# First weights transformed by kind, the gate's transfer issued behind the first fold, and four sums ahead of two folds

## The chip, the cores and the metric

The kernel runs on one core of a Trainium2 chip. The metric is the device time of one execution in microseconds (us); smaller is better. The core has five engines that run in parallel, each with its own instruction queue worked through in order: TensorE (PE, matrix products into the PSUM memory), VectorE (DVE), ScalarE (ACT), GpSimd (POOL) and SyncE (SP, which here only issues transfers). DMA transfers are issued by SP, ACT or POOL and are carried out by 16 DMA engines that all issuers share.

## The reference

```python
def _attn_ref(x):                     # x: (8, 3008, 256) f32
    X = np.fft.fft(x, axis=1)
    X = np.fft.fft(X, axis=2)
    return X.real.astype(np.float32)

def _moe_ref(x, w_gate, w_val, w_out):  # (24064, 256), two (256, 1536), (1536, 256)
    g = x @ w_gate
    silu = g * (1.0 / (1.0 + np.exp(-g)))
    val = x @ w_val
    return (silu * val @ w_out).astype(np.float32)
```

The real part of a two-dimensional Fourier transform of each of 8 sequences is flattened to 24,064 rows and goes through a gated feed-forward block (SwiGLU) with inner width 1536.

## The kernel before, in words

The transform along the 256 columns is moved into the weights: the gate and value weights are multiplied once by a cosine table (`CD`) and a sine table (`SDt`). This gives `Wp` (cosine kind) and `Wq` (sine kind), and `Wm`, which is `Wq` scaled by `m2` for the mirrored rows. The transform along the 3008 rows is done on PE with tables `Tab`, after the rows have been "folded": rows and columns that share a cosine or sine are added or subtracted first. Its results are the tiles `Pt` and `Qt`. Then the long steady loop takes `Pt` and `Qt` through `Wp`, `Wq` and `Wm` (line 1337 on PE), SiLU and products on ACT, DVE and POOL, and the output weights (line 1599 on PE). The order of that loop is fixed by a planner when the kernel is built; it is the same whatever happens before it. The change lies in the code ahead of the loop, which is written out by hand in the order of the queues; it prepares the first sequence and the first 512 of the 1536 columns of the gate and value weights.

The first sequence is loaded in two chunks: a long one (`XA`, 128 row groups) and a short one (`XC0`, 60 row groups twice). SP and ACT issue the loads of x; POOL issues the weights, which are cast to bf16 on the way.

- `load_w` (lines 394 and 396): four transfers issued by POOL. `load_w(1, (0,))` is the first 512 columns of the gate into `W0[0]`, `load_w(1, (1,))` those of val into `W0[1]`, and `load_w(0)` the other 1024 columns of both into the space of `XA`.
- `place` (line 444): PE brings rows into order; `sums` (line 453): DVE adds or subtracts these and the rows that fall, into `SA` (long chunk) and `SC` (short chunk).
- `fold_d` (lines 511, 512): POOL folds `SA` over the columns, one quarter of it a call, and ACT casts the result to `EOb`. `fold_c` (line 507): DVE folds `SC` into `EB` (named `EOf` in the profile).
- `half_folded` (line 497) and `folded_c` (line 503): PE accumulates the first transform out of the long and the short chunk into four accumulators: `eo` 0 gives `Pt`, 1 gives `Qt`, each with one in a `v` and one in a `g` slot of PSUM. `row0` (line 611) adds single rows to those of `Qt`.
- `transform` (lines 642, 647): ACT copies one accumulator, and DVE adds and subtracts it from the other into `Pt` or `Qt`.
- `half_w` (lines 473, 475, 477): the first 512 weight columns in two halves of 256. A call makes one kind (cosine or sine) for gate and val together: four products into one PSUM tile of the `o` slots, and one copy, on ACT or (second half, cosine kind) on DVE. `double` (line 481): ACT makes `Wm` of one half.
- `weight_op` (lines 1805, 1808, 1811, 1814): the first operations of the loop that need the other 1024 columns.
- `opposite` (line 383), `weigh_ce` (line 386): ACT finishes tables. `turns` (line 363, POOL) and `angles` (line 367, DVE) start the tables for a later part. At line 669 ACT clears a small tile that SP then writes into the empty rows of `XC` (line 671).

PSUM has 8 slots: three named `g`, three `v`, two `o`; each kind is handed out in turn ahead of the loop, and by the planner inside it.

Of the kernel before, what the change touches and what calls it, by code (L numbers as in the profile page):

```python
# [12 lines left out]
F32 = mybir.dt.float32  # L13
I32 = mybir.dt.int32
BF16 = mybir.dt.bfloat16
AF = mybir.ActivationFunctionType
# [15 lines left out]
def kernel(  # L32
# [8 lines left out]
    nc = tc.nc  # L41
    B, M, D = x.shape
    Dff = moe_w_gate.shape[1]
    P = 128
# [5 lines left out]
    T = 512  # L50
# [42 lines left out]
    psG = Slots("psG", 3, space=bass.MemoryType.PSUM)  # L93
    psV = Slots("psV", 3, space=bass.MemoryType.PSUM)
    psO = Slots("psO", 2, space=bass.MemoryType.PSUM)
    ctx.enter_context(tc.manual_schedule())

    Wp = const.tile([P, 2, Dff], BF16, name="Wp")
    Wq = const.tile([P, 2, Dff], BF16, name="Wq")
    Wm = const.tile([P, 2, Dff], BF16, name="Wm")  # L100
# [6 lines left out]
    CD = const.tile([P, 2, P], BF16, name="CD")  # L107
    SDt = const.tile([P, 2, P], BF16, name="SDt")
    m2 = const.tile([P, 1], F32, name="m2")
# [135 lines left out]
    SC = tq.tile([P, 2, 2, 2, D], F32, name="SC")  # L245
    SA = tp.tile([P, 2, 4, 2, D], F32, name="SA")
    EOb = tp.tile([P, 2, 4, 2, P], BF16, name="EOb")
    XC0 = tp.tile([P, 4, 2, D], F32, name="XC0")
    W0 = [tp.tile([P, 2, T], BF16, name=f"W0{i}") for i in range(2)]
# [8 lines left out]
    q = nc.sync  # L258
# [48 lines left out]
    for i in range(4):  # L307
        ps = psO.tile([P, T], F32, name="o")
# [46 lines left out]
    def row_signs():  # L355
        pts(sgo, pc, scalar1=float(NCR), scalar2=-2.0, op0=Alu.is_equal, op1=Alu.mult)
        pts(sgo, sgo, scalar1=1.0, scalar2=sgn, op0=Alu.add, op1=Alu.mult)
# [18 lines left out]
    def cosine(ch, lo, hi, ra):  # L376
        nc.scalar.activation(Tab[:, ch, :, 0, lo:hi], ra, AF.Sin, scale=-sc, bias=halfpi)
# [4 lines left out]
    def opposite(ch):  # L382
        nc.scalar.activation(Tab[:, ch, :, :, NCE:NOO - 1], Tab[:, ch, :, :, GH + 1:NCE], AF.Copy, scale=-1.0)
# [4 lines left out]
    def load_w(first, only=(0, 1)):  # L388
        for i, src in ((0, moe_w_gate), (1, moe_w_val)):
            if i not in only:  # L390
                continue
            w_ = src.rearrange("(no p) f -> p no f", p=P)
            if first:
                nc.gpsimd.dma_start(out=W0[i], in_=w_[:, :, 0:T])
            else:
                nc.gpsimd.dma_start(out=Wraw[i][:, :, 0:Dff - T], in_=w_[:, :, T:Dff])
# [13 lines left out]
    nc.gpsimd.memset(EOf[:, 1, :, P:P + 1], 0.0)  # L410
    nc.gpsimd.memset(sel[0:1, :], 1.0)
    row_signs()
    load_w(1, (0,))


    ce_angle = [[tp.tile([P, 2, NCE], F32, name=f"{nm}{ch}") for nm in ("rr", "ra")] for ch in range(2)]
# [32 lines left out]
    def sums(S, k, X, pss, only=None):  # L449
        n = len(pss)  # L450
        for a in only or range(n):
            down = X[:, 7 - a] if n == 4 else X[:, 2 + a]
            vtt(S[:, k, a], pss[a], down[:, ::-1, :], op=(Alu.add, Alu.subtract)[k])
# [10 lines left out]
        for i in range(n):  # L464
            nc.tensor.matmul(ps[:, 0:P], sel, sel, start=True, stop=True)

    def half_w(h, k, pool, nm):
        ps = pool.tile([P, 2, T // 2], F32, name=nm)
        dst, tab = ((Wp, CD), (Wq, SDt))[k]
        fs = slice(h * T // 2, (h + 1) * T // 2)  # L470
        for gv in range(2):
            for no in range(2):
                nc.tensor.matmul(ps[:, gv, :], tab[:, no, :], W0[gv][:, no, fs], start=(no == 0), stop=(no == 1))
        if k or not h:
            nc.scalar.copy(dst[:, :, fs], ps)
        else:
            nc.vector.tensor_copy(dst[:, :, fs], ps)

    def double(h):
        fs = slice(h * T // 2, (h + 1) * T // 2)  # L480
        nc.scalar.activation(Wm[:, :, fs], Wq[:, :, fs], AF.Copy, scale=m2)

    def start_acc(eo):
        for q, (pool, nm) in enumerate(((psV, "v"), (psG, "g"))):
            acc[eo][q] = pool.tile([P, T], F32, name=nm)

    def set_cols(ps, tab, a):
        if a % 2:
            return (ps[:, 0:2 * GH + 2].rearrange("p (t n) -> p t n", t=2),
                    tab[:, 0:2 * NCE].rearrange("p (t n) -> p t n", t=2)[:, :, 0:GH + 1])  # L490
        return ps[:, 0:NCE], tab[:, 0:NCE]

    def half_folded(eo, a0):
        for q in range(2):
            for a in range(a0, a0 + 2):
                dst, rhs = set_cols(acc[eo][q], Tab[:, 0, q, eo], a)
                nc.tensor.matmul(dst, EOb[:, eo, a, q, :], rhs, start=(a == 0), stop=False, skip_group_check=True)

    def folded_c(eo):
        for a in range(2):  # L500
            for q in range(2):
                dst, rhs = set_cols(acc[eo][q], Tab[:, 1, q, eo], a)
                nc.tensor.matmul(dst, EB[:, eo, a, q, :], rhs, start=False, stop=a == 1, skip_group_check=True)

# [4 lines left out]
    def fold_d(eo, a0):  # L509
        s_ = SA[:, eo, a0:a0 + 2]  # L510
        ptt(EOA[:, eo, a0:a0 + 2, :, 0:P], s_[:, :, :, P:0:-1], s_[:, :, :, P:D], op=(Alu.add, Alu.subtract)[eo])
        nc.scalar.copy(EOb[:, eo, a0:a0 + 2], EOA[:, eo, a0:a0 + 2, :, 0:P])
# [34 lines left out]
    start_acc(1)  # L547
    start_acc(0)
    fold_d(0, 0)
    cosine(1, 0, NCE, ce_angle[1][1])  # L550
    half_folded(0, 0)
    psC = place(XC0, putC, 2, ((psO, "o"),))
# [6 lines left out]
    load_w(0)  # L559
    opposite(1)  # L560
    half_folded(0, 2)
    half_folded(1, 2)
    for k, a in ((0, 0), (1, 0), (0, 1)):
        sums(SC, k, XC0, psC, (a,))
    fold_c(0)
    sums(SC, 1, XC0, psC, (1,))
    fold_c(1)
    X3c = XC.rearrange("p a q d -> p (a q d)")
    hd = tp.tile([P, 2, 2, 1], F32, name="hd")
# [31 lines left out]
    def row0(b, q, ps):  # L601
        CE = coef_a(b)[0]
        if b:
            for k, (c, e) in enumerate(((0, E0), (0, E1), (1, slice(0, NCE)))):
                nc.tensor.matmul(ps[:, e], Z0[:, q, k, :], Tab[:, c, q, 0, e], start=False, stop=True,  # L605
                                 skip_group_check=True)
            return
        todo = [(CE[:, q, 0, k, P:P + 1], Tab[:, 0, q, 0, e], e) for k, e in ((0, E0), (1, E1))]
        todo += [(CEc[:, q, 0, k, 0:1], Tab[:, 1, q, 0, e], e) for k, e in ((0, E0), (1, E1))]
        for l, r_, cols in todo:  # L610
            nc.tensor.matmul(ps[0:1, cols], l, r_, start=False, stop=True, skip_group_check=True)
# [11 lines left out]
    def transform(b, part, eos, given=None):  # L623
        n = NCE if part == 0 else G
        ev, ods = {}, {}
        for q, pool, nm in ((0, psO, "o"), (1, psG, "g")):
            if given:
                ps = {eo: given[eo][q] for eo in eos}
            else:
                ps = {eo: pool.tile([P, T], F32, name=nm) for eo in eos}  # L630
                for eo in eos:
                    mms = products(b, part, q, eo)
                    for i, (l, r_, cols) in enumerate(mms):
                        nc.tensor.matmul(ps[eo][:, cols], l, r_, start=(i == 0), stop=(i == len(mms) - 1),
                                         skip_group_check=True)
            if part == 0 and 1 in eos and not given:

                row0(b, q, ps[1])
            for eo in eos:
                if q == 0:  # L640
                    ods[eo] = odp.tile([P, NCE], F32, name="od")
                    nc.scalar.copy(ods[eo][:, 0:n], ps[eo][:, 0:n])
                else:
                    ev[eo] = ps[eo]

        def put(eo, dst, s0, w, minus):
            nc.vector.tensor_tensor(dst, ev[eo][:, s0:s0 + w], ods[eo][:, s0:s0 + w],
                                    op=Alu.subtract if minus else Alu.add)

        if part == 0:  # L650
            runs = [(0, GH, 1, 0), (GH, GH, 0, 1), (G, GH, GH + 1, 0), (G + GH, GH, GH + 1, 1)]
        else:
            runs = [(2 * G, G, 0, 0), (3 * G, G, 0, 1)]
        todo = []
        for eo in eos:
            for c0, n_, s0, minus in runs:
                for t, off, src, w in pieces(b * H + c0, n_):
                    todo.append((t, eo, off, s0 + src, w, minus))
        for t, eo, off, s0, w, minus in sorted(todo, key=lambda v: v[0:2]):
            put(eo, pq_tiles(t)[eo][:, off:off + w], s0, w, minus)  # L660
        if part == 0:
            for eo in eos:
                put(eo, last[eo][:, b:b + 1], 0, 1, 0)
# [6 lines left out]
    for hi in range(2):  # L670
        q.dma_start(out=X3c[64 * hi + NCR:64 * hi + 64, :].rearrange("p (c d) -> p c d", d=D),
                    in_=zeros[64 * hi + NCR:64 * hi + 64].unsqueeze(1).to_broadcast([64 - NCR, 16, D]))
    folded_c(0)
    transform(0, 0, (0,), acc)
    angles(rrO[:, 0], kfO, 0, rrO[:, 0].bitcast(I32), (0,))
    for k in range(2):
        half_w(0, k, psO, "o")
    folded_c(1)
    for i in range(2):
        row0(0, i, acc[1][i])  # L680
    transform(0, 0, (1,), acc)
    double(0)
    for k in range(2):
        half_w(1, k, psO, "o")
    double(1)
    turns(rrO[:, 1].bitcast(I32), kfO, 1)
    E_, O_ = EOA[:, 0].rearrange("p a q d -> p q a d"), EOA[:, 1].rearrange("p a q d -> p q a d")
# [1340 lines left out]
```

## Time and profile before

| | us |
|---|---|
| median of 3 runs | 601.02 (600.91 to 601.09) |
| the profiled execution | 601.23 |
| its span, from the first to the last instruction | 599.5 |
| PE busy in the stretches 10 to 15, 15 to 20, 20 to 25 (5 us each) | 4.25, 4.55, 5.00 |
| DVE busy in the same | 4.18, 4.61, 4.79 |
| ACT busy in the same | 4.24, 3.83, 4.58 |
| POOL busy in the same | 4.88, 4.81, 4.88 |
| granted clock of PE, mean | 0.999 |

Times inside the profile count from the first instruction. A line such as `L507` is a line of the kernel's source. Operations of one engine overlap a little, so a row's duration can be longer than the distance to the next one on the same engine. What a row shows in brackets is the time in which its engine was idle just before it, and what ended that.

### The profile page before, as it was taken

How to read it: one execution, taken by the hardware profiler on the slowest of the kernel's cores; microseconds unless marked ns; L12 is line 12 of the kernel's file. 1: busy time of each engine (PE TensorE's matmuls, PEld its weight loads, DVE VectorE, ACT ScalarE, POOL GpSimd, SP SyncE). 2: the span in 40 equal slices, each digit the busy share in tenths (PEclk: the TensorE clock that was granted, in tenths of full speed). 3: DMA queues.
4: the chain of work that ended last, by engine and by line, in shares of the span. 5: the costliest groups of instructions: out<-in, count | busy, mean ns of one | idle time of the engine just before them, and what ended most of it. 6: DMA issues, size and time to landing. Idle time of an engine off the chain costs nothing.

```text
span 599.5 us, 12541 instructions
## 1 busy us (share of the span) xinstructions
PE 591.4 (99%) x4027; PEld 390.7 (65%) x4027; DVE 572.2 (95%) x1058; ACT 562.5 (94%) x1090; POOL 515.2 (86%) x464
## 2 busy tenths in 40 slices
PE   8999999999999999999999999999999999999996
PEld 5556666666666666666666666666666666666685
DVE  8989998999999999999999999999999999999993
ACT  8899999999989999899999999998999899999994
POOL 9738999999799999999999988997899557787772
PEclk9999999999999999999999999999999999999999
DMA  9946347354716414354245112045111211211112
GB/s 241 151 99 139 114 119 184 88 131 120 191 38 129 119 52 125 109 131 137 63 90 150 36 54 74 19 122 173 45 62 37 63 46 55 61 43 42 59 54 80
DMA packets 50555, 57.65 MB, mean 96 GB/s; under 512 B 7267, under 2 KB 37399, under 8 KB 50489
## 3 DMA queue, kind: packets, MB, share of 16 engines
q1 hardware_dynamic: 47529, 53.97, 33.5%
q0 software_dynamic: 2672, 2.36, 2.6%
q8 instruction: 31, 0.51, 0.4%
q10 hardware_dynamic: 288, 0.52, 0.3%
q14 instruction: 35, 0.29, 0.2%
HBM read 29.43 MB, written 24.65 MB: 90 GB/s over the span
## 4 chain that ended last, share of the span: by engine, by line
PE 90%; DMA 3%; DVE 3%; ACT 1%; issue 1%; SPq 1%; POOL 1%; ACTq 0%; DVEq 0%; POOLq 0%
PE o L1599 38%; PE g L1337 25%; PE v L1337 20%; PE g L1757 2%; PE o L1757 2%; DMA XC<-in_x_dram 1%; DMA XA<-in_x_dram 1%; DVE sv L1540 1%; DVE es L1474 1%; PE v L1599 1%; PE o L1805 1%; DVE hp L1551 1%; SPq L171 0%; POOL SDf L189 0%; PE g L605 0%
## 5 line engine op out<-in xcount | busy, mean ns | idle before, releaser
L1548 POOL TENSOR_TENSOR hm<-sv 128x1024 bf16<-128x1024 f32 (+2 forms) x137 | 254.8, 1862 | 49.2 <-DVE sv L1540 21.4
L1540 DVE SCALAR_TENSOR_TENSOR sv<-es,v 128x512 f32<-128x512 f32 (+2 forms) x262 | 175.0, 672 | 7.3 <-PE v L1337 5.1
L1599 PE MATMUL o<-Wo,hm 128*128 128x256 bf16 (+1 forms) x1128 | 163.2, 273 | 0.0
L1551 DVE TENSOR_TENSOR hp<-sp,v 128x512 bf16<-128x512 f32 (+2 forms) x236 | 157.8, 672 | 2.0 <-PE v L1337 1.3
L1599 PE MATMUL o<-Wo,hp 128*128 128x256 bf16 (+1 forms) x1104 | 159.3, 272 | 0.0
L1599 PEld LDWEIGHTS <-hm 128*128 128x128 bf16 (+2 forms) x1140 | 111.8, 98 | 57.4 <-issue 1.0
L1599 PEld LDWEIGHTS <-hp 128*128 128x128 bf16 (+2 forms) x1140 | 111.9, 98 | 54.7 <-issue 1.3
L1524 ACT ACTIVATE sv<-g 128x512 f32<-128x512 f32 (+2 forms) x178 | 117.9, 674 | 4.2 <-PE g L1337 3.1
L1449 ACT ACTIVATE sp<-g 128x512 f32<-128x512 f32 (+2 forms) x178 | 111.0, 625 | 4.6 <-PE g L1337 2.3
L1337 PE MATMUL g<-Pt,Wp 128*128 128x512 bf16 (+2 forms) x288 | 107.5, 374 | 0.0
L1410 ACT ACTIVATE v<-bc,w 128x512 f32<-128x512 bf16 (+2 forms) x147 | 105.8, 722 | 1.1 <-DVE hp L1551 0.6
L1337 PE MATMUL v<-Pt,Wp 128*128 128x512 bf16 (+2 forms) x288 | 106.4, 375 | 0.0
L1337 PE MATMUL g<-Qt,Wq 128*128 128x512 bf16 (+2 forms) x288 | 104.6, 375 | 0.0
L1472 ACT ACTIVATE es<-v 128x512 f32<-128x512 f32 (+2 forms) x147 | 90.9, 623 | 4.5 <-PE v L1337 2.3
L1474 DVE SCALAR_TENSOR_TENSOR es<-bc,w,v 128x512 f32<-128x512 bf16 (+2 forms) x127 | 93.4, 737 | 1.1 <-ACT bc L1932 0.2
L1337 PEld LDWEIGHTS <-Wp 128*128 128x128 bf16 x576 | 56.3, 98 | 27.2 <-issue 0.9
L1337 PE MATMUL g<-Qt,Wm 128*128 128x512 bf16 (+2 forms) x192 | 72.2, 376 | 0.1
L1453 DVE SCALAR_TENSOR_TENSOR sg<-bc,w,g 128x512 f32<-128x512 bf16 (+2 forms) x96 | 69.6, 725 | 0.3 <-PE g L1337 0.2
L1524 ACT ACTIVATE sv<-sg 128x512 f32<-128x512 f32 (+2 forms) x96 | 66.6, 699 | 0.4 <-DVE sg L1517 0.4
L1521 ACT ACTIVATE sp<-g 128x512 f32<-128x512 f32 (+2 forms) x96 | 59.2, 617 | 6.0 <-DVE sg L1517 5.6
L1517 DVE SCALAR_TENSOR_TENSOR sg<-sg,g 128x512 f32<-128x512 f32 (+2 forms) x96 | 63.7, 664 | 0.5
L1337 PE MATMUL v<-Qt,Wm 128*128 128x512 bf16 (+2 forms) x161 | 60.0, 373 | 0.0
(196 smaller groups left out, 758.7 us busy)
## 6 DMA issues: line engine op xcount, KB each, us to landing
out_dram<-ev SPq DMA_DIRECT2D x96, 128.0 KB
XA<-in_x_dram SPq DMA_DIRECT2D x30, 256.0 KB
XA<-in_x_dram SPq DMA_DIRECT2D x112, 64.0 KB
XC<-in_x_dram SPq DMA_DIRECT2D x28, 120.0 KB
XC<-in_x_dram SPq DMA_DIRECT2D x105, 32.0 KB
bc<-br SPq DMA_DIRECT2D x19, 128.0 KB
St<-Fc SPq DMA_DIRECT2D x12, 128.5 KB
out_dram<-ev SPq DMA_DIRECT2D x12, 120.0 KB
```

The costliest lines, as they stand in the source:

```text
L1337: nc.tensor.matmul(ps[:, :n], Wt[:, gv, fs], src[:, :n], start=start, stop=stop, skip_group_check=True)
L1410: nc.scalar.activation(T_[kv][:, :w], bc[t][:, :w], AF.Copy, scale=w0[:, 1, f:f + 1])
L1449: nc.scalar.activation(sp_to()[:, :w], T_[kg][:, :w], AF.Silu)
L1453: nc.vector.scalar_tensor_tensor(T_[keg][:, :w], bc[t][:, :w], w0[:, 0, f:f + 1], T_[kg][:, :w], op0=Alu.mult, op1=Alu.add)
L1472: nc.scalar.activation(T_[kes][:, :w], T_[kv][:, :w], AF.Copy, scale=2.0 if on_pool(u) > 1 else 1.0)
L1474: nc.vector.scalar_tensor_tensor(T_[kes][:, :w], bc[t][:, :w], w0[:, 1, f:f + 1], T_[kv][:, :w], op0=Alu.mult, op1=Alu.add)
L1517: nc.vector.scalar_tensor_tensor(T_[kgm][:, :w], T_[keg][:, :w], 2.0, T_[kg][:, :w], op0=Alu.mult, op1=Alu.subtract)
L1524: nc.scalar.activation(sv()[:, f % 2, w - 1::-1, 1], T_[kgm if by_dve else kg][:, :w], AF.Silu)
L1540: nc.vector.scalar_tensor_tensor(sv()[:, f % 2, w - 1::-1, 0], T_[kes][:, :w], 2.0, T_[kv][:, :w], op0=Alu.mult, op1=Alu.subtract)
L1548: nc.gpsimd.tensor_tensor(hts_(t)[1][:, f - 1:f + 1, :w], sv()[:, :, :w, 1], sv()[:, :, :w, 0], op=Alu.mult)
L1551: nc.vector.tensor_tensor(hts_(t)[0][:, f, :wp], T_[ksp][:, :wp], T_[kv][:, :wp], op=Alu.mult)
L1599: nc.tensor.matmul(st["ps"][:n, j, :], hts[t][minus][:, f, c:c + n], Wo[:, f, :], start=(f == 0), stop=(f == nF - 1))
```

## The change

The gate's first transfer is issued by POOL behind the first `fold_d` instead of ahead of all folds. `half_w` is replaced by `first_w`, which makes one kind of one matrix over all 512 columns: two products into one PSUM tile and one copy, always on ACT. The gate's cosine kind goes into a `v` slot between two `half_folded` calls, the gate's sine kind into a `g` slot and val's two kinds into `o` slots. `double` now goes by matrix. Of the short chunk, all four sums stand ahead of its two folds. `folded_c(1)` and `row0` are done for one accumulator after the other.

```diff
@@ tables and first transfers
     row_signs()
-    load_w(1, (0,))
@@
-    def half_w(h, k, pool, nm):
-        ps = pool.tile([P, 2, T // 2], F32, name=nm)
-        dst, tab = ((Wp, CD), (Wq, SDt))[k]
-        fs = slice(h * T // 2, (h + 1) * T // 2)
-        for gv in range(2):
-            for no in range(2):
-                nc.tensor.matmul(ps[:, gv, :], tab[:, no, :], W0[gv][:, no, fs], start=(no == 0), stop=(no == 1))
-        if k or not h:
-            nc.scalar.copy(dst[:, :, fs], ps)
-        else:
-            nc.vector.tensor_copy(dst[:, :, fs], ps)
-
-    def double(h):
-        fs = slice(h * T // 2, (h + 1) * T // 2)
-        nc.scalar.activation(Wm[:, :, fs], Wq[:, :, fs], AF.Copy, scale=m2)
+    def first_w(gv, k, pool, nm):
+        ps = pool.tile([P, T], F32, name=nm)
+        tab = (CD, SDt)[k]
+        for no in range(2):
+            nc.tensor.matmul(ps, tab[:, no, :], W0[gv][:, no, :], start=(no == 0), stop=(no == 1))
+        return lambda: nc.scalar.copy((Wp, Wq)[k][:, gv, 0:T], ps)
+
+    def double(gv):
+        nc.scalar.activation(Wm[:, gv, 0:T], Wq[:, gv, 0:T], AF.Copy, scale=m2)
@@
-    def folded_c(eo):
+    def folded_c(eo, qs=(0, 1)):
         for a in range(2):
-            for q in range(2):
+            for q in qs:
@@
     fold_d(0, 0)
+    load_w(1, (0,))
     cosine(1, 0, NCE, ce_angle[1][1])
     half_folded(0, 0)
@@
     half_folded(0, 2)
+    gate_p = first_w(0, 0, psV, "v")
     half_folded(1, 2)
-    for k, a in ((0, 0), (1, 0), (0, 1)):
+    for k, a in ((0, 0), (1, 0), (0, 1), (1, 1)):
         sums(SC, k, XC0, psC, (a,))
     fold_c(0)
-    sums(SC, 1, XC0, psC, (1,))
     fold_c(1)
@@
     folded_c(0)
+    gate_p()
     transform(0, 0, (0,), acc)
     angles(rrO[:, 0], kfO, 0, rrO[:, 0].bitcast(I32), (0,))
-    for k in range(2):
-        half_w(0, k, psO, "o")
-    folded_c(1)
+    copies = [first_w(0, 1, psG, "g"), first_w(1, 0, psO, "o")]
+    for c in copies:
+        c()
     for i in range(2):
+        folded_c(1, (i,))
         row0(0, i, acc[1][i])
     transform(0, 0, (1,), acc)
     double(0)
-    for k in range(2):
-        half_w(1, k, psO, "o")
+    first_w(1, 1, psO, "o")()
     double(1)
```

## The prediction

> **What bounds the kernel now.** I read the page first, then the timeline from 8 to 37 us by engine, then the DMA view cut into windows of 1 us, then the waits of TensorE after 20 us.
>
> ```profile
> span 599.5 us, 12541 instructions
> PE 591.4 (99%) x4027; PEld 390.7 (65%) x4027; DVE 572.2 (95%) x1058; ACT 562.5 (94%) x1090; POOL 515.2 (86%) x464
> ```
>
> TensorE (PE) is busy for 591 of 599.5 us, and after 40 us it has hardly a wait. The edits all lie in the first 21 us, before the steady loop, so the question is only by how much the loop starts earlier or later. The timeline around that start (start us, us, engine, line, operation; in brackets the idle time before it and what ended it):
>
> ```profile
> 20.85 0.37 PE L1337 MATMUL v<-Pt,Wp 128*128 128x480 bf16 x1
> 20.93 0.25 PEld L1805 LDWEIGHTS <-CD 128*128 128x128 bf16 x2 [0.18 <-DMA XA<-in_moe_w_gate_dram]
> 21.06 0.72 ACT L481 ACTIVATE Wm<-Wq,m 128x512 bf16<-128x512 bf16 x1
> 21.08 0.59 PE L1805 MATMUL o<-XA,CD 128*128 128x512 bf16 x2
> ...
> 21.51 0.36 PE L1337 MATMUL g<-Qt,Wq 128*128 128x480 bf16 x1
> ...
> 21.96 1.03 ACT L1372 ACTIVATE sg<-g 128x480 f32<-128x480 f32 x2 [0.17 <-PE g L1337]
> ```
>
> The loop's first four products (L1337 at 20.24 to 20.85, spaced 0.20) are followed in PE's order by the first product on the rest of the gate weights (L1805). Its weight load started at 20.93, the moment that transfer landed; 0.12 us later it would have held PE up (the fourth product leaves the array at 20.85 + 0.20 = 21.05). Behind it in PE's queue stand all products with Qt, and the first SiLU on ScalarE (ACT) waits for one of these (21.96). From 21.96 to 37.2 the timeline shows ACT without a gap, and at 36.5 to 36.9 PE waits for it. So a late first SiLU is paid in full at the end. The thing to follow is when that transfer is issued. It is issued by GpSimd (POOL):
>
> ```profile
> 8.16 0.82 POOL L394 DMA_DIRECT2D W<-in_moe_w_gate_dram  x1
> 9.26 2.27 POOL L511 TENSOR_TENSOR EOA<-SA 128x512 f32<-128x512 f32 x2 [0.29 <-DVE SA L453]
> 11.47 0.73 POOL L394 DMA_DIRECT2D W<-in_moe_w_val_dram  x1
> 12.23 2.14 POOL L511 TENSOR_TENSOR EOA<-SA 128x512 f32<-128x512 f32 x2
> 14.30 0.73 POOL L396 DMA_DIRECT2D XA<-in_moe_w_gate_dram  x1
> 15.03 0.73 POOL L396 DMA_DIRECT2D XA<-in_moe_w_val_dram  x1
> 15.77 0.57 POOL L570 TENSOR_TENSOR hd<-SA 128x4 f32<-128x4 f32 x1
> ```
>
> POOL has no idle time from 9.26 on. At 8.16 the gate's issue fell into time in which POOL would have waited for the sums anyway. Last, the short chunk on VectorE (DVE):
>
> ```profile
> 12.77 1.29 DVE L453 TENSOR_TENSOR SC<-o,XC 128x512 f32<-128x512 f32 x2
> ...
> 14.87 0.69 DVE L453 TENSOR_TENSOR SC<-o,XC 128x512 f32<-128x512 f32 x1 [0.81 <-DMA XC<-in_x_dram]
> ...
> 15.59 0.69 DVE L507 TENSOR_TENSOR EOf<-SC 128x512 bf16<-128x512 f32 x1
> ...
> 16.20 0.68 DVE L453 TENSOR_TENSOR SC<-o,XC 128x512 f32<-128x512 f32 x1
> ...
> 16.92 0.70 DVE L507 TENSOR_TENSOR EOf<-SC 128x512 bf16<-128x512 f32 x1
> ```
>
> Its third sum waits 0.81 us for the last rows of x. The windows say why. From 9 to 12 us the SP queue (q1) moves about 155 packets a microsecond; from 12 to 13 the gate's packets of POOL's queue (q0) take over, 164 against 38 of q1, and from 13 to 14 it is 133 against 73. The last x transfer was issued by SP at 8.52, after the gate's at 8.16, and went behind it.
>
> **The change part by part.**
>
> **The gate's issue, 8.16 to behind the first fold.** The first fold doesn't start earlier, since it waits for the sums (9.26). It ends at 10.35, and an issue follows a fold 1.03 us after the fold's start (12.23 + 1.08 for the second pair's first fold, 13.27 to 14.30), so the gate is issued at 10.30. An issue holds POOL for 0.75 (11.47 to 12.23). The second fold then starts at 11.04 instead of 10.45: between the two folds stood 0.15 us of waiting for DVE that pays for part of it. From there on POOL is late by 0.59: val's issue 12.07, folds 12.82 and 13.87, the rest of the gate 14.89, the rest of val 15.62, the small operations from 16.36. The casts of the folds on ACT (L512, 0.62 each, 0.03 behind the fold) come at 12.2, 13.95 and 15.0 instead of 11.73, 13.36 and 14.40, and the table negation behind them (L383, 0.83) at 15.5 instead of 14.93.
>
> **The x rows.** Without 512 KB of gate weights (256 KB as landed) ahead of it, the last x transfer follows its predecessors: 113 packets of q1 are left at 12.0, at 155 a microsecond 0.7 us, and landing came about 0.7 after the last packets (those of 13 to 14 us, landed at 14.74). So it lands at about 13.4. The third sum then waits for PE's placing product instead (L444, until 13.89) and starts at 13.98, 0.89 earlier.
>
> **Four sums, then the folds.** Independent sums follow each other at 0.60 (9.09, 9.69), a fold on a fresh sum at 0.72 (14.87, 15.59). So: sums 13.98 and 14.58, folds 15.19 and 15.79, ended 15.9 and 16.5 instead of 16.28 and 17.62. Were the x rows no earlier, the first fold would start at 16.07 instead of 15.59, the second at 16.68 instead of 16.92; that costs PE 0.4, which the wait found below covers.
>
> **The first weights by kind.** Before: 16 products of 256 columns (L473), 0.87 and 0.88 us as two blocks (17.00 to 17.87, 19.36 to 20.24). After: eight of 512 at 0.43 a pair (L1805, 21.08 to 21.51). PE's time stays 1.75, but one pair moves into PE's idle time near 15.5 and only one stays behind the row products, which saves 0.45 there. The gate's pair now stands in PE's queue ahead of the last half-fold (L497), so the gate must have landed by then. Bounds: val took 4.2 us from issue to landing, the gate 6.4 with q1's packets ahead of it. After 10.30 that is 14.5 or 16.7. I take 14.5 to 14.9, as q1's backlog is nearly gone by 12.4. PE reaches the pair at 15.3, so it is covered by 0.4 us.
>
> PE then goes: half-fold 14.65 to 15.3 (0.65, L497 14.37 to 15.02), gate pair to 15.75, last half-fold (its cast ends at 15.65) to 16.4, short chunk (L503, 0.66; its first table-negated operand is ready at 16.35) to 17.1, two pairs to 17.95, then short chunk and row products by accumulator, 0.33 + 0.09 + 0.33 twice (L503 18.52 and L611 18.61 to 19.27), to 19.5, last pair to 19.95. The loop starts at 19.97 instead of 20.24, a gain of 0.27.
>
> **The copies.** ACT takes four copies of 0.58 (spaced 0.48) instead of three, DVE loses one of 0.68. ACT: the gate's first copy at about 16.95 delays the even accumulator's copy (L642) from 17.04 to 17.4; two copies 17.8 and 18.3, the odd accumulator's copy at 18.9 instead of 19.14, doubling 19.3, last copy 20.17 instead of 20.45, doubling until 21.5. DVE's Qt puts come at about 19.7 (19.64 before), after the angles (L367), whose POOL operand comes 0.59 late at 18.75 and is still in time. Qt's first tile is complete at 20.45. All this lies before 21.5.
>
> **The rest of the gate.** Issued 0.59 late, it lands 0.59 late if the transfer takes the 6.6 us of before. The wait of L1805 then runs to 20.93 + 0.59 = 21.52, while PE stands ready at 19.97 + 0.81 = 20.78. The product followed its load by 0.15 before, with the array just coming free; with an idle array short-chunk products followed theirs at once (16.34 both). So it starts between 21.53 and 21.67 instead of 21.08: +0.45 to +0.59, and I take **+0.5**. Everything gained ahead of it, 0.27 on PE and 0.89 on DVE, is swallowed by this wait of 0.75 us. Val's rest lands at 24.6 instead of 24.0 and is needed at 24.17 + 0.5: no further loss. What POOL does behind it (0.59 late until 23.2) has cover: its next operation waits for ACT's Wq copy, and the output weights, landed at 34.7, are used at 39.8. The zero fill that SP issues behind ACT's L669 (16.44) slips with it, which moves the second batch's x loads by as much as the loop itself moves.
>
> **Sum.** The profiled execution took 601.23 us, a span of 599.5 and 1.73 around it. With +0.5 the span is 600.0 and the execution 601.7; the median of the runs shown, 601.02, lies 0.21 below that execution, so **601.5**. A measurement of this kernel can tell about 0.2%, 1.2 us, from no change.
>
> **Rivals.**
>
> **The transfer is not late (600.75).** Of the 6.6 us only 2.6 are data at the 0.2 MB a microsecond of the windows from 17 to 20, and within the 18 to 19 window falls one 16 KB packet of the instruction queue, which can hold one of the 16 engines up by about a microsecond. If the slower first stretch (46 and 53 GB/s from 15 to 17) or this packet falls away, it lands by 20.8, PE doesn't wait, and the gain of 0.27 stands. Against it: PE's instruction count reaches the same place at about the same time, so the packet should fall into the transfer again. In the Trainium skill, DMA: Bandwidth & Descriptors, section Anatomy of one DMA — SWDGE (gpsimd) path, such a transfer takes about 2.0 us plus its bytes over 436 GB/s; an estimate by it is 3.2 us for 512 KB, landing at 18.1, hence this rival. By that rule the transfer of before would not have held L1805, and the trace, with 6.6 us, disagrees. Chance 0.2.
>
> **The gate comes late at its new place (602.2).** If it takes the 6.4 us of before, or the 6.6 of its rest, it lands at 16.7 or 16.9, and PE, in order, holds the last half-fold, the short chunk and all behind it for it. From 16.75: pair to 17.2, half-fold 17.85, short chunk 18.5, two pairs 19.35, accumulators 20.9, last pair and loop start 21.35, L1805 at 22.2 instead of 21.08: +1.1, with 16.9 +1.3. It decides over the forecast from a landing at 16.1. For it: both large transfers of POOL took over 6 us. Against it: the gate's own 6.4 were spent behind packets that have gone by then. Chance 0.2.
>
> That the change does not bring the x rows earlier alters nothing, as shown: PE would reach L1805 at 21.15, still before 21.52.
>
> **How the numbers follow.** Forecast 0.6 (+0.3 to +0.8), not late 0.2 (-0.3 to 0), late gate 0.2 (+1.0 to +1.5). The range 600.6 to 602.3 takes in the first two and most of the third. Faster by over 0.2% would need 1.2 us, and PE's whole gain is 0.27: 0.04, for things not seen. Slower by over 0.2%: the upper half of the late gate and a little beside it, 0.15. The rest, 0.8, is within.
>
> **What would show it.** POOL: L394 gate at 10.3, second fold at 11.0, L396 at 14.9. DVE: no wait in front of the third sum for x, folds at 15.2 and 15.8. PE: the gate pair near 15.3 to 15.8 without a DMA wait, loop products from 20.0, and in front of L1805 a wait of about 0.75 us for the DMA; first SiLU at 22.4. Wrong would be no wait there, or one in front of the gate pair.

## The result, and the profile after

| | changed kernel | before, same chip |
|---|---|---|
| median, us (22 runs each) | 602.06 (601.32 to 602.93) | 601.15 (600.73 to 601.88) |
| ratio, 95% interval | 1.0017 [1.0011, 1.0022] | |
| the profiled execution, us | 601.62, span 599.8 | 601.23, span 599.5 |

The changed kernel is slower by 0.91 us. That lies within the 0.2% named ahead of the runs and within the range given, but it is nearly twice the +0.5 of the sum. The profiled execution is among the quicker ones of the changed kernel (0.44 below its median), so its profile shows less of the loss than the median: its last instruction ends 0.39 later than before.

The page of the changed kernel, its head:

```profile
span 599.8 us, 12526 instructions
PE 592.3 (99%) x4019; PEld 390.2 (65%) x4019; DVE 571.6 (95%) x1057; ACT 563.0 (94%) x1091; POOL 514.7 (86%) x464
```

PE has eight matmuls fewer (the first weights) and is as full as before. What was edited runs ahead of 25 us, so the reading starts there. POOL's timeline of the changed kernel (start, us, engine, line, operation; idle time in brackets):

```profile
9.07 1.09 POOL L504 TENSOR_TENSOR EOA<-SA 128x512 f32<-128x512 f32 x1 [0.86 <-DVE SA L452]
10.11 0.81 POOL L394 DMA_DIRECT2D W<-in_moe_w_gate_dram  x1
10.94 1.10 POOL L504 TENSOR_TENSOR EOA<-SA 128x512 f32<-128x512 f32 x1
11.98 0.73 POOL L394 DMA_DIRECT2D W<-in_moe_w_val_dram  x1
12.73 2.14 POOL L504 TENSOR_TENSOR EOA<-SA 128x512 f32<-128x512 f32 x2
14.81 0.73 POOL L396 DMA_DIRECT2D XA<-in_moe_w_gate_dram  x1
15.54 0.72 POOL L396 DMA_DIRECT2D XA<-in_moe_w_val_dram  x1
```

The gate's issue now stands between two folds, and both transfers of the rest are issued 0.51 later than before (14.30, 15.03). Counted from the first fold, which starts at 9.07 here and at 9.26 before, it is 0.70. In all profiles of this document that fold starts between 9.05 and 9.59, with the gate early or late; so the times of two single profiles compare only to some tenths of a microsecond. DVE's timeline of the changed kernel has the short chunk without a gap:

```profile
12.58 2.48 DVE L452 TENSOR_TENSOR SC<-o,XC 128x512 f32<-128x512 f32 x4
14.98 1.28 DVE L500 TENSOR_TENSOR EOf<-SC 128x512 bf16<-128x512 f32 x2
```

The wait of 0.81 us for x is gone. PE's timeline of the changed kernel, from the gate's pair to the first product on val's rest:

```profile
15.19 0.59 PE L470 MATMUL v<-W,CD 128*128 128x512 bf16 x2
...
19.90 0.37 PE L1332 MATMUL g<-Pt,Wp 128*128 128x480 bf16 x1
...
21.30 0.60 PE L1800 MATMUL o<-XA,CD 128*128 128x512 bf16 x2 [0.43 <-DMA XA<-in_moe_w_gate_dram]
...
24.20 0.37 PE L1332 MATMUL v<-Qt,Wm 128*128 128x480 bf16 x1
24.61 0.59 PE L1800 MATMUL o<-XA,CD 128*128 128x512 bf16 x2
```

The last two of these in the kernel before:

```profile
23.97 0.37 PE L1337 MATMUL v<-Qt,Wm 128*128 128x480 bf16 x1
24.17 0.59 PE L1805 MATMUL o<-XA,CD 128*128 128x512 bf16 x2
```

The loop starts at 19.90, 0.34 earlier than before. PE then stands idle for the rest of the gate, and the first product on it is 0.22 later than before (21.30 against 21.08). At the first product on the rest of val 0.44 is lost (24.61 against 24.17): without a wait it would follow the product at 24.20 after 0.20, as before. The chain of waits of the changed kernel between 14 and 26 us, in order of time (start, us, what), names the reason:

```profile
13.83 1.04 POOL EOA L504
14.87 0.66 POOL XA L396
15.54 9.03 DMA XA<-in_moe_w_val_dram
24.57 0.04 issue
24.61 0.59 PE o L1800 x2
```

The rest of val, issued at 15.54, lands 9.03 us later, at 24.57. PE loses 0.21 on it in this execution, on top of the 0.22 on the gate's rest. Before, val's rest is in no link of the same chain: it goes from the late x over DVE's sums and PE's products to 25 us without a break.

### The profile page after: what moved, and what is told of

It reads as the page before. It is cut to its first block, busy times and chain, and to the rows that moved or that the text cites. A ratio compares the mean times of both kernels' runs of the same rounds, so it can differ in the third digit from the quotient of the medians.

```text
span 599.8 us, 12526 instructions
## 1 busy us (share of the span) xinstructions
PE 592.3 (99%) x4019; PEld 390.2 (65%) x4019; DVE 571.6 (95%) x1057; ACT 563.0 (94%) x1091; POOL 514.7 (86%) x464
## 4 chain that ended last, share of the span: by engine, by line
PE 88%; DMA 4%; DVE 2%; POOL 2%; ACT 1%; issue 1%; SPq 1%; ACTq 0%; DVEq 0%; POOLq 0%
PE o L1594 38%; PE g L1332 25%; PE v L1332 19%; PE g L1752 2%; PE o L1752 2%; DMA XA<-in_moe_w_val_dram 2%; DMA XA<-in_x_dram 1%; DVE sv L1535 1%; POOL EOA L504 1%; PE v L1594 1%; DVE es L1469 1%; DVE hp L1546 1%; PE o L1800 0%; SPq L171 0%; DMA XC<-in_x_dram 0%
```

## The experiments

The question was where the other 0.4 us of the loss are. Theory A puts the loss on POOL: its weights are issued later and land later, first the rest of the gate, then that of val. Against it stood the other parts of the change (the first weights' form, the order of the sums), and from the first profiles on rival E: the chain over DVE's second angles operation (L367), the first `hp` (DVE) and PE's product `v<-Qt,Wm`. Kernels of one group ran on one chip, beside the kernel before. In the diffs the lines are the edits against the kernel named.

### Group 1: one part undone, or alone (before: 601.55)

**Gate's issue back** (changed kernel):

```diff
+    load_w(1, (0,))          # behind row_signs(), as before
     fold_d(0, 0)
-    load_w(1, (0,))
```

> The changed kernel with one part undone: POOL issues the gate's first transfer ahead of all folds again. Theory A (the loss is the late issue of the remaining weights): L396 back at 14.3, the remaining gate lands near 20.9; the x rows land at 14.8 again, sums at 14.87 and 15.47, folds at 16.1 and 16.7, loop start near 20.35, first L1800 near 21.15 with little or no wait for the DMA: +0.1 us on before, 601.0 to 601.5. Rival B (the loss is the rearranged first weights: four copies on ACT, other PSUM slots, another instruction stream on PE): it stays, about 602.0.

**Only the gate's issue moved** (kernel before): the same two lines the other way round.

> The kernel before with one part of the change alone: the gate's first transfer is issued behind the first fold. Theory A: L396 at 14.8 to 14.9, loop start about where it was (20.2), then a wait for the DMA in front of L1805 until 21.3 to 21.6 and perhaps a second one for val: +0.4 to +0.9 us, 601.6 to 602.1. Rival B: no loss, 601.15.

**Only the first weights by kind** (kernel before, with `first_w`, `folded_c(1, (i,))` and `double` of the change):

> The kernel before with one part alone: first weights by matrix and kind (with the accumulators one after the other), gate issue and sums as before. Theory A: loop start near 20.0, then held by the landing at 20.9, L1800 between 20.95 and 21.1: -0.1 to 0 us, 601.0 to 601.2. Rival B: the whole loss, about 602.0.

**POOL 0.7 us later still** (changed kernel):

```diff
     fold_d(1, 2)
+    nc.gpsimd.memset(pad[:, 0:752], 0.0)
     load_w(0)
```

> The changed kernel with the suspected cost doubled: POOL clears 752 columns of an unused f32 tile (about 0.7 us by the clear of 752 columns at L1876) between the last fold and L396, so only the remaining weights are issued later, at 15.5. The output stays that of the reference. Theory A: the wait in front of L1800 grows by the same 0.7 us and so does the time, to about 602.8. Rival B: nothing waits for it, 602.06.

| kernel | median, us | ratio, 95% interval |
|---|---|---|
| gate's issue back | 601.87 | 1.0006 [0.9997, 1.0015] |
| only the gate's issue | 602.22 | 1.0013 [1.0005, 1.0022] |
| only the first weights | 601.50 | 0.9998 [0.9989, 1.0007] |
| POOL later still | 602.71 | 1.0021 [1.0012, 1.0029] |

The move of the gate's issue is the part that costs: +0.67 alone, with an interval clear of no change, and the loss falls from 0.91 to 0.32 when it is undone (the two intervals overlap). The first weights by kind show neither cost nor gain in the median: their profile starts the loop at 19.67 (before 20.24), and PE stands before the rest of the gate until 21.10 (before 21.08). The chain of waits of that kernel (window 11 to 26 us):

```profile
13.49 1.03 POOL EOA L505
14.53 6.53 DMA XA<-in_moe_w_gate_dram
21.05 0.05 issue
21.10 0.60 PE o L1801 x2
```

A gain ahead of that transfer is swallowed there, as the prediction had it. With the gate's issue back but the rest of the change (the profile is the quickest of its 11 runs, 601.28), the rest of the gate is issued at 14.10 and PE meets it at 20.61, 0.47 earlier than before and without a wait. Yet nothing of that is left at 24 us. The same view of that kernel shows a third thing that holds the loop there:

```profile
21.85 0.28 DVE XA L367
22.13 1.07 issue
23.19 0.65 DVE hp L1370
23.84 0.04 issue
23.89 0.36 PE v L1332
```

The angles operation of DVE, which takes 0.60 where nothing is in its way, is followed by `hp` only 1.34 after its start; PE's `v<-Qt,Wm` waits for that `hp` until 23.89 (before 23.97). This is rival E's chain. In the kernel with only the gate's issue moved it holds too: `hp` at 24.06, `v<-Qt,Wm` at 24.76, first product on val's rest at 24.96.

In that profile theory A has no part: PE finds both rests landed, the gate's when it comes to it at 21.47. What is late there is the loop start, 20.64 against 20.24, and its chain of waits (window 11 to 26 us) shows another road from the issue to PE:

```profile
10.68 0.75 POOL W L394
...
13.24 2.15 POOL EOA L510 x2
...
15.42 0.63 ACT EOb L511
...
16.09 0.50 PE v L496 x2
```

The issue holds up POOL's folds, and the cast of the last fold holds PE's last half-fold (16.09, before 15.07). Of the 0.40 at the loop start, the first fold brings 0.33 with it (9.59 in this execution). So this kernel shows that the move costs, but not that it costs through the rest of the weights. In the changed kernel the gate's pair covers this road: its last half-fold follows the pair without a wait.

### Group 2: the changed kernel again, and POOL's last fold on DVE (before: 601.36)

**The changed kernel again**, and **POOL later still again**, the two side by side:

> The changed kernel as it is, beside the others of this call. Theory A, sharpened: the first product on val's remaining weights is what decides, since in the runs so far that transfer's last packets come 8.6 to 8.9 us after the issue of the remaining gate and the product starts about 1.0 us behind them. With L396 at 14.8 to 14.9 that product starts at 24.5 to 24.7 instead of 24.17: +0.4 to +0.9 us on before.

> The clear of 752 columns on POOL ahead of the remaining weights again, now on the chip of the changed kernel. Theory A, sharpened: +0.7 us on the changed kernel. Rival C (only the wait for the remaining gate counts, and that one ended early in the first look, at 21.19): within 0.2 us of the changed kernel.

**The changed kernel with POOL's last fold on DVE**, ahead of the four sums, so that POOL can issue the rest earlier:

```diff
-    def fold_d(eo, a0):
+    def fold_d(eo, a0, tt=ptt):
...
-    fold_d(1, 2)
+    fold_d(1, 2, vtt)
```

> The changed kernel with POOL's last fold (L511 in before, eo 1, second half) moved to DVE, ahead of the four sums, so POOL issues the remaining weights 1.03 us earlier, near 13.8. Theory A, sharpened: val's rest is there by 23.5, nothing waits, the gain on PE (0.27 to 0.34 at the loop start) comes through: -0.2 to -0.4 us on before, and -0.6 to -1.3 on the changed kernel. Rival B (the rearranged first weights cost the time): still +0.7 to +0.9 on before.

**The same fold on DVE, with the gate's issue and the order of the sums as before** (changed kernel):

```diff
+    load_w(1, (0,))          # behind row_signs(), as before
     fold_d(0, 0)
-    load_w(1, (0,))
...
-    fold_d(1, 2)
+    for k in range(2):
+        sums(SC, k, XC0, psC, (0,))
+    fold_d(1, 2, vtt)
...
-    for k, a in ((0, 0), (1, 0), (0, 1), (1, 1)):
-        sums(SC, k, XC0, psC, (a,))
+    sums(SC, 0, XC0, psC, (1,))
     fold_c(0)
+    sums(SC, 1, XC0, psC, (1,))
     fold_c(1)
```

> First weights by matrix and kind as in the change, gate issue ahead of all folds and order of sums and folds as before, and the last fold of the long chunk on DVE in the time in which DVE waits for x. Theory A, sharpened: L396 near 13.3 to 13.5, no wait for either remaining transfer, loop start near 19.7 to 20.0: -0.3 to -0.5 us on before.

| kernel | rest of gate issued | first product on gate's rest, on val's rest | median, us | ratio, 95% interval |
|---|---|---|---|---|
| before | 14.30 | 21.08, 24.17 | 601.36 | |
| changed again | 15.05 | 21.41, 25.31 | 602.27 | 1.0019 [1.0010, 1.0027] |
| POOL later still | 15.79 | 21.50, 25.55 | 602.51 | 1.0020 [1.0011, 1.0029] |
| changed, last fold on DVE | 14.35 | 21.51, 24.84 | 602.14 | 1.0011 [1.0002, 1.0020] |
| order of before, last fold on DVE | 13.48 | 21.09, 24.89 | 600.99 | 0.9997 [0.9988, 1.0006] |

The loss of 0.91 came again. This profile of the changed kernel has both waits, and the second is the larger. Its PE timeline:

```profile
21.41 0.61 PE L1800 MATMUL o<-XA,CD 128*128 128x512 bf16 x2 [0.30 <-DMA XA<-in_moe_w_gate_dram]
24.31 0.37 PE L1332 MATMUL v<-Qt,Wm 128*128 128x480 bf16 x1
25.31 0.59 PE L1800 MATMUL o<-XA,CD 128*128 128x512 bf16 x2 [0.64 <-DMA XA<-in_moe_w_val_dram]
```

and its chain of waits (window 11 to 26 us):

```profile
15.10 0.67 POOL XA L396
15.78 9.50 DMA XA<-in_moe_w_val_dram
25.27 0.04 issue
25.31 0.59 PE o L1800 x2
```

Its last instruction ends 1.12 later than before, near the 1.14 by which the product on val's rest is late. So in two executions of one kernel the second wait cost 0.2 and 0.8.

That the end is as late as PE was at 25 us is a coincidence, though. Near 75 us ACT waits 0.43 for DVE's `sg` in the first profile of the changed kernel, and from there its operations are 0.35 later against before. All nine profiles with the first weights by kind and POOL's last fold in place show this step (0.30 to 0.37), and none of the other four does (at most 0.02); the nine have one DVE instruction fewer than before. In the two profiles of the changed kernel about as much comes back behind 80 us, in three steps, the last at the very end. No run settles what sets these steps.

But "issued later, landed later" in equal measure is not borne out. The 0.74 that the clear put on POOL's issue cost 0.24 in the median, and where the rest was issued 0.7 and 1.6 earlier (last two rows) val's rest took 9.72 and 10.64 us and landed at 24.8 both times, later than the 24.57 of the first profile. (The median of the last row is nevertheless 0.37 under the kernel before, as theory A had forecast, and 1.28 under the changed kernel; that of the row above, for which 0.2 to 0.4 under before was forecast, is 0.78 above. The profiles of these two rows lie 0.67 above and 0.63 below their medians and can't say why.) The transfers in flight between 15 and 25 us share the 16 DMA engines, and it is the last of these that ends them. In the changed kernel run again 15 of the engines had written their last packet of val's rest by 23.71 and the sixteenth at 24.86; in the first profile it was 23.43 and 23.66.

### Group 3: the rest in halves (before: 601.28)

**The rest in four transfers**, those of columns 512 to 1023 (`fc=1`) at the old place and those of 1024 to 1535 (`fc=2`) behind a later copy on POOL, in the changed kernel, in the kernel with only the first weights, and in the kernel before:

```diff
-    load_w(0)
+    load_w(0, fc=1)
...
     nc.gpsimd.tensor_copy(EOA[:, 0, :, :, P:P + 1], SA[:, 0, :, :, 0:1])
+    load_w(0, fc=2)
```

> The changed kernel with the remaining weights in four transfers instead of two: columns 512 to 1023 of gate and val at the old place, columns 1024 to 1535 issued by POOL after the small copy at L575 of before (near 19). What PE needs first is then half as long and has nothing behind it in the same transfer. Theory A' (the time goes into PE's waits for the last engine of the remaining transfers, above all val's, and scatters with it): no wait in front of the first products on either, the gain of 0.3 us at the loop start stays: 0 to -0.5 us on before, about -1.2 on the changed kernel. Rival B (rearranged first weights) and rival D (the moved issue costs somewhere else, such as val's first transfer): still +0.7 to +0.9 on before.

> First weights by matrix and kind, gate issue and sums as before, and the remaining weights in four transfers. Theory A': loop start 19.7 to 20.0 and no wait after it: -0.2 to -0.6 us on before. Rival B: at or above before.

> The kernel before with the remaining weights in four transfers and nothing else. Theory A': PE was just in time in the profiled execution of before, so there is little to gain in most executions and something in those in which the transfer was late: 0 to -0.3 us on before.

| kernel | loop start | products on gate's and val's rest | median, us | ratio, 95% interval |
|---|---|---|---|---|
| changed, halves | 19.88 | 20.72, 25.33 | 602.71 | 1.0022 [1.0012, 1.0031] |
| first weights, halves | 19.26 | 20.10, 24.15 | 601.69 | 1.0007 [0.9998, 1.0016] |
| before, halves | 19.45 | 20.29, 24.18 | 601.54 | 1.0005 [0.9996, 1.0014] |

Half the bytes land early enough that no first product waits for a DMA: 20.10 to 20.72 instead of 21.08 to 21.41. Nothing of it reaches 24 us, and none of the three gains that theory A' forecast came. DVE's and POOL's timelines of the changed kernel with halves show why:

```profile
21.95 2.56 DVE L367 SCALAR_TENSOR_TENSOR XA<-XA,mM 128x376 f32<-128x376 f32 x1
24.44 1.20 DVE L1372 TENSOR_TENSOR hp<-sg,v 128x480 bf16<-128x480 f32 x2
...
21.60 1.27 POOL L685 TENSOR_TENSOR BBa<-EOA 128x512 bf16<-128x512 f32 x1
22.84 1.26 POOL L686 TENSOR_TENSOR BBa<-EOA 128x512 bf16<-128x512 f32 x1
```

The angles operation starts 0.35 behind POOL's `BBa` and ends at 24.51, 0.41 behind the end of the second one; `hp` and PE's `v<-Qt,Wm` (25.13) wait for it. In the kernel with POOL later still (group 1) the order was the other way, and DVE's operation is short and POOL's long:

```profile
22.43 0.60 DVE L367 SCALAR_TENSOR_TENSOR XA<-XA,mM 128x376 f32<-128x376 f32 x1
...
22.55 1.63 POOL L685 TENSOR_TENSOR BBa<-EOA 128x512 bf16<-128x512 f32 x1
```

The Trainium skill, SBUF — State Buffer, section Who interferes with whom, has the rule for it: a DVE instruction with two inputs in SBUF and a GpSimd instruction that reads SBUF exclude each other for a whole instruction, and whichever is first wins. The traces agree, with 2.56 and 0.60 us for the one and 1.27 and 1.63 for the other. So an earlier product on the gate's rest brings DVE's operation into POOL's `BBa`. How many of POOL's operations it waits for then counts. In the first weights with halves (DVE, then POOL):

```profile
21.34 2.00 DVE L367 SCALAR_TENSOR_TENSOR XA<-XA,mM 128x376 f32<-128x376 f32 x1
...
21.65 1.27 POOL L686 TENSOR_TENSOR BBa<-EOA 128x512 bf16<-128x512 f32 x1
...
22.89 1.57 POOL L687 TENSOR_TENSOR BBa<-EOA 128x512 bf16<-128x512 f32 x1
```

DVE's operation starts 0.31 ahead of the first `BBa`, while an earlier operation of POOL still runs, and is through 0.42 behind the end of that `BBa`; the second one takes longer. The kernel before with halves is alike (1.84 us). In these two PE is back at 24.15 and 24.18, the time of before (24.17), from a lead of 0.8 to 1.0. In the changed kernel, where DVE's operation comes behind the start of `BBa` and waits for both, PE is 1.2 behind. No version is clearly faster than the kernel before. The profiles of the first two rows are the slowest execution of their kernel: the first weights with halves lost 1.4 us more between 165 and 200 us, and the changed kernel with halves about 0.5 near 85 and 0.6 between 165 and 200 us; why stays open.

### Group 4: only val's rest split (before: 601.42)

**The changed kernel with the rest of val in two** (`lo` and `hi` bound its columns): its first half at the old place, its second behind `BBa`, so that POOL's times up to there stay:

```diff
-    load_w(0)
+    load_w(0, (0,))
+    load_w(0, (1,), hi=T)
...
     ptt(BBa[:, :, 1, :, 0:1], E_[:, :, 3::-3, P:P + 1], E_[:, :, 1:3, P:P + 1], op=Alu.subtract)
+    load_w(0, (1,), lo=T)
```

> The changed kernel with val's rest in two transfers: columns 512 to 1023 at the old place, columns 1024 to 1535 issued by POOL right behind the last of BBa. POOL's time up to BBa stays, only the transfer that the first product on val's rest needs is shorter. Theory A' (that transfer's slowest DMA engine lands last and sets the end): it lands about 1.3 us earlier, the first product on val's rest has no wait on a DMA (24.4 at the latest, instead of 24.6 to 25.3), and the kernel is 0.2 to 0.4 us above the one before; the second half is needed at about 28.4 and lands at about 27.5, and a wait near 28.5 would show if it is late. Rival E (the chain over DVE's angles op, the first hp and v<-Qt,Wm sets the end): v<-Qt,Wm stays at 24.2 to 24.4 and the kernel stays 0.7 to 0.9 us above the one before. No part of the computation is left out.

602.26 us, 1.0014 [1.0005, 1.0023]: +0.84, not the 0.2 to 0.4 of theory A'. The median is the one that rival E asked for, but its row isn't: `v<-Qt,Wm` comes at 24.71, not at 24.2 to 24.4. The PE timeline has no second wait:

```profile
21.81 0.61 PE L1802 MATMUL o<-XA,CD 128*128 128x512 bf16 x2 [0.78 <-DMA XA<-in_moe_w_gate_dram]
24.71 0.37 PE L1334 MATMUL v<-Qt,Wm 128*128 128x480 bf16 x1
24.91 0.59 PE L1802 MATMUL o<-XA,CD 128*128 128x512 bf16 x2
```

The product on val's rest follows the one before it by 0.20. What it should have gained stands elsewhere. The rest of the gate, issued at 14.96, took 6.80 us in this execution and cost 0.73 by itself. Then DVE's timeline has two operations that are longer than before:

```profile
24.71 1.17 DVE L371 TENSOR_SCALAR SDf<-XA 128x752 int32<-128x752 int32 x1
27.48 1.55 DVE L367 SCALAR_TENSOR_TENSOR XA<-XA,mM 128x376 f32<-128x376 f32 x2
```

Before, these take 0.54 and 1.12. Both lie beside work that POOL does later here because of the added issue (the output weights' issue from 24.46, `Wm` from 27.54); that POOL stretched them is read from the rows of group 3, whose DVE operation has two inputs in SBUF where L371 has one, and wasn't tried. ACT then waits 0.33 for the `hp` behind them, and the shift of ACT's operations against the kernel before goes from +0.76 to +1.18 at 28.5 us. So the mechanism (val's rest holds PE) is shown by the two profiles of the changed kernel and by its absence here, but its share of the median is not: without it the loss is 0.84 against 0.91, which the intervals don't tell apart.

## Why the prediction was right, point by point

- **POOL late by one issue: right in kind, 0.11 too small.** Forecast 0.59 for the rest, measured 0.51 (14.81); but the first fold came 0.19 earlier than before, which the sum had at its old place, and from it the delay is 0.70. The sum let the gate's issue hold POOL for 0.74, as val's did; it held POOL for 0.83 (10.11 to 10.94). That the 0.51 is so near the 0.59 is luck; the second profile, with the fold at 9.31, has 0.75.
- **x rows, sums and folds: right.** Third sum at 13.79 without a wait (forecast 13.98), folds at 14.98 and 15.6 (15.19 and 15.79).
- **The gate at its new place: right.** It took 4.1 us instead of 6.4 and landed at 14.2 (forecast 14.5 to 14.9); the pair ran at 15.19 with no wait. The rival in which the gate comes late fell.
- **The loop start: right**, 19.90 for 19.97 (20.13 in the second profile), and **its gain swallowed: right**; the first weights alone start the loop 0.57 earlier and gain nothing in the median.
- **The wait in front of the rest of the gate: right in place, smaller in the first profile.** Forecast +0.45 to +0.59; +0.22 and +0.33 in the two profiles of the changed kernel, since the transfer took 6.4 and 6.3 us and not the 6.6 of before, +0.73 where it took 6.80. The first SiLU follows at 22.19 (forecast 22.4). The rival without a late transfer fell: PE waited in each profile of the changed kernel.
- **"Val's rest lands at 24.6 instead of 24.0 and is needed at 24.17 + 0.5: no further loss": this step failed.** The landing was right in the first profile (24.57), where PE needed it at 24.4: the two waits together, 0.44, are then no more than the +0.5 of the sum. What was wrong is that a cover of less than 0.1 us (24.6 against 24.67) counted as enough. The step took one transfer time, 9.0 us, for all executions; the changed kernel shows 9.0 and 9.5, and over all kernels that issue this transfer whole it is 8.8 to 10.6. In the second profile the rest landed at 25.27 and was needed at 24.5, which is a further 0.8.
- **The term that was mis-sized** is therefore the +0.5: +0.91 in the median (interval +0.66 to +1.3, from the ratio). Of it, +0.59 goes with the gate's issue by the difference to the kernel with that put back (each against its own before), and the remaining 0.32 is within that kernel's interval (-0.2 to +0.9). How the 0.91 divides between the rest of the gate, the rest of val and DVE's chain is not settled: each profile is one execution, and not the same one comes last in all of them.
- **The range held partly by luck.** +0.91 lies between the +0.3 to +0.8 of the forecast and the +1.0 to +1.5 of the late gate, a rival that the traces rule out. The range takes 602.06 in because it was drawn over both.

## What to carry to other kernels

A DMA issue put ahead of a queue's work costs everything behind it in that queue its time (0.70 us here), operations and issues alike, so weigh it by the last of them, not by the one that is moved. Where several transfers, an engine's chain and a shared port are all due within half a microsecond, removing one wait brings out the next; look for the floor by removing them together. And one landing time from one profile is a sample: where the cover is below its scatter, put the loss into the sum and not only into the range.

## What the runs showed of the hardware

- **A DVE operation with two SBUF inputs took 0.60 to 2.56 us** by how many of POOL's operations on SBUF, of 1.27 us each, it waited for (group 3). Where it waited, it was through about 0.41 behind the end of the last of them. The single-input one at L371 took 0.54 or 1.17 (group 4).
- **A transfer beside another queue's backlog took longer.** The gate's first 256 KB took 6.4 us when issued at 8.16, beside the loads of x, and 4.1 when issued at 10.11; the last x transfer then no longer held up the third sum.
- **An instruction fetch may set the end of a transfer.** One 16 KB packet of the instruction queue takes 0.9 to 1.2 us of one DMA engine (0.95 in most profiles). In the kernel before, 15 of the 16 engines had landed their share of the gate's rest by 19.91 and the sixteenth at 20.89; in the first profile of POOL later still all sixteen landed between 20.79 and 21.14. Where it fell at 16.8, ahead of most of the stream (the two kernels with POOL later still), the rest of the gate took 5.4 and 5.7 us; at 17.8 to 19.0 (the changed kernel twice, and three others) 6.3 to 6.6; at 19.7 to 19.8 (three kernels) 6.8 to 7.6. One kernel goes against it (20.05 and 5.8). It wasn't tried by itself. The Trainium skill's estimate for such a transfer, 3.2 us (DMA: Bandwidth & Descriptors, section Anatomy of one DMA — SWDGE (gpsimd) path), is not met by any of them.
